# The first loads in another order, and a conv group of two blocks, in a fused convolution and gated feed-forward kernel

## The chip, the cores and the metric

One core of a Trainium2 chip runs the kernel. The metric is the device time of one execution in microseconds (us), lower is better. Times of the kernel before are the median of four runs.

## What is computed

The kernel computes a lightweight causal convolution over the sequence (seven taps, eight heads of 24 channels, softmax-normalised weights) and feeds it into a feed-forward layer whose activation is h * cos(h).

```
def _attn_ref(x, weight):                # x: 8 x 4096 x 192, weight: 8 heads x 7 taps
    w = np.exp(weight - np.max(weight, axis=-1, keepdims=True))
    w = w / (np.sum(w, axis=-1, keepdims=True) + 1e-09)
    x_pad = np.concatenate([np.zeros((B, K - 1, D)), x], axis=1)
    x_unf = x_pad[:, np.arange(S)[:, None] + np.arange(K)[None, :], :].reshape(B, S, K, H, group)
    return np.einsum('hk,bskhg->bshg', w, x_unf).reshape(B, S, D)

def _moe_ref(x, w_in, w_out):            # 32768 tokens x 192; 192 x 2048; 2048 x 192
    h = x @ w_in
    return (h * np.cos(h)) @ w_out
```

## The kernel before

**Two lanes.** The eight batch rows are split in two: lane 0 holds rows 0 to 3 in partitions 0 to 63, lane 1 rows 4 to 7 in partitions 64 to 127. A matmul of 64 rows in one lane runs beside one in the other; `lanes` (L282) interleaves two lists of such matmuls. In what follows "batch b" is the pair of rows b and b + 4.

**The convolution.** A batch has 4096 tokens, cut in 37 blocks of 112. `load_blocks` (L104 to L110) loads up to four neighbouring blocks of x, as overlapping windows of 64 tokens, into a staging tile of the pool `xw`, which has eight buffers; it issues one DMA for each lane, on the queues that it is given (SyncE's, unless said). A *conv pair* is a list of up to eight slots, each one block and one of the three chunks of 64 channels. `cast` (L157) copies the slots of a pair to bf16 (`xb`), on GpSimd unless said. `conv_first` multiplies them with the banded tap matrix (`band`), head by head: a pair whose slots are all of one chunk has 12 or 16 matmuls, one that has slots of all three chunks has 40. `evacuate` (L338, L340) copies the result to SBUF (`ct`), and `conv_out` issues a DMA transpose on SyncE (L367), which writes the conv result channel-major to `cT`. The list `pairs` gives the order of the pairs and `loads` that of the loads. Before, batch 0 is cut in groups of 5, 8, 8, 8, 8 blocks, and the others in 8, 8, 8, 8, 5. A group of eight makes three pairs, a group of five makes two; there are 56 pairs in all. Pairs 0 and 1 (the first five blocks) are transposed by TensorE (L482), not by DMA.

**The feed-forward part.** A *step* covers 512 tokens in both lanes and 128 of the 2048 hidden units. `up` (letter U) makes h from `w1` and `cT` with six matmuls in a PSUM tile `h`; `sin` (S, L387) takes the cosine on ScalarE; `mult` (M, L392) multiplies on VectorE into `g`. Sixteen steps make a tile of tokens, and steps 16 n and on read tile n. `down` (d) multiplies `g` with `w2` into the two accumulator banks `acc`, eight matmuls at a time; sixteen d make a *set* (one lane's half of a tile's output), so that there are 64 sets, with eight U in each. In a set the two lanes change banks three times. At each change a *lane mark* is needed: a memset of one element on GpSimd (L292) that waits for the d before it, and the next d waits for the mark. GpSimd works in the order in which its instructions are written, so what stands ahead of a mark on GpSimd delays it. `store` (x, y, L429) copies the accumulators out.

**The start.** The order is written out by hand. First `loads[0]` (blocks 0 to 3) and `loads[1]` (block 4), the softmax of the taps, the quarters of w_in (`load_w1`, L226 and L228, cast in L231), `loads[2]` and `loads[3]` (blocks 5 to 12), and the halves of w_out (`load_w2`, L236, cast in L241). All weights go through the same eight staging tiles. Then a string of letters is emitted by `fill`, in which each k takes the next job from the list `later()`: a cast of weights, a `cast_pair`, or a `load_ahead`. `load_ahead(n)` issues loads until the blocks of the n-th next pair are under way. With `load_ahead(4)` the loads are issued on SyncE ahead of the transposes of pairs 2, 3 and 4, which make the tokens of tile 1. Then each set is one string: `C` and `c` are the two halves of a pair's conv, `e` its copy and transposes, and `p` is `cast_pair` and `load_ahead()`. In set 1 a second pair is convolved (`CcpdMSeU`), since tile 2 needs all of pairs 5, 6 and 7.

Of the kernel before, what the change touches and what calls it, by code (L numbers as in the profile page):

```python
# [16 lines left out]
def kernel(  # L17
# [21 lines left out]
    nc = tc.nc  # L39
    B, S, D = x.shape  # L40
    H, K = weight.shape
    Dff = moe_w_in.shape[1]
# [6 lines left out]
    L = 64  # L49
    NCH = D // L  # L50
# [4 lines left out]
    NBLK = (S + W - 1) // W  # L55
# [5 lines left out]
    def dram(ap, offset, dims):  # L61
        return bass.AP(tensor=ap.tensor, offset=offset, ap=dims)
# [21 lines left out]
    def staging(dims):  # L84

        n = math.prod(dims)
        t = xw_pool.tile([128, 2 * NB * D], FP32, name="xw")[:, 0:n]
        names = "abc"[:len(dims)]
        return t.rearrange(f"p ({' '.join(names)}) -> p {' '.join(names)}", **dict(zip(names, dims)))


    lane = (slice(0, L), slice(L, 128))

    def load_blocks(b, k0, n, queues=(nc.sync, nc.sync)):

        xw = staging([2 * n, D])
        if k0 + n == NBLK:
            nc.gpsimd.memset(xw[:, 2 * n - 1, :], 0.0)
        for s, queue in enumerate(queues):
            base = ((s * HB + b) * S + k0 * W - BEFORE) * D  # L100
            w0, w1 = 0, 2 * n
            if k0 == 0:
                nc.gpsimd.memset(xw[s * L:s * L + BEFORE, 0, :], 0.0)
                queue.dma_start(out=xw[s * L + BEFORE:(s + 1) * L, 0, :], in_=dram(x, base + BEFORE * D, [[D, V], [1, D]]))  # L104
                w0 = 1
            if k0 + n == NBLK:
                w1 -= 1
                rows = TAIL - V + BEFORE
                queue.dma_start(out=xw[s * L:s * L + rows, w1, :], in_=dram(x, base + w1 * V * D, [[D, rows], [1, D]]))
            queue.dma_start(out=xw[lane[s], w0:w1, :], in_=dram(x, base + w0 * V * D, [[D, L], [V * D, w1 - w0], [1, D]]))  # L110
        for k in range(k0, k0 + n):
            xws[b, k] = xw, k - k0


    pairs = []
    loads = []
    for b in range(HB):
        five = 0 if b == 0 else NBLK - 5
        for k in range(0 if five else 5, NBLK - (5 if five else 0), 8):
            pairs += [[(b, k + j, c) for j in range(8)] for c in range(NCH)]  # L120
            loads += [(b, k, 4), (b, k + 4, 4)]
        both = [[(b, five + j, c) for c in range(2) for j in range(4)],
                [(b, five + 4, c) for c in range(NCH)] + [(b, five + j, 2) for j in range(4)]]
        if five:
            pairs += both
            loads += [(b, five, 4), (b, five + 4, 1)]
        else:
            pairs = both + pairs
            loads = [(b, five, 4), (b, five + 4, 1)] + loads
    NC = len(pairs)  # L130
    xbs = {}

# [14 lines left out]
    def cast(p, copies=(nc.gpsimd.tensor_copy,)):  # L147

        xbs[p] = xb_pool.tile([128, 8, 2, L], BF16, name="xb")
        for j, (s0, s1) in enumerate(runs(pairs[p])):  # L150
            b, k, c = pairs[p][s0]
            xw, k0 = xws[b, k]
            if s1 - s0 > 1 and pairs[p][s0 + 1][1] == k:
                src = xw[:, 2 * k0:2 * k0 + 2, :].rearrange("p w (c l) -> p c w l", l=L)
            else:
                src = xw.rearrange("p (k w) c -> p k w c", w=2)[:, k0:k0 + s1 - s0, :, c * L:(c + 1) * L]
            copies[j % len(copies)](out=xbs[p][:, s0:s1], in_=src)  # L157
# [25 lines left out]
    nc.vector.memset(band, 0.0)  # L183


    load_blocks(*loads[0])
    wmax = consts.tile([KB, H], FP32)
    nc.vector.tensor_reduce(out=wmax, in_=wq, axis=AX.X, op=ALU.max)
    nc.vector.tensor_tensor(out=wq, in0=wq, in1=wmax.unsqueeze(2).to_broadcast([KB, H, K]), op=ALU.subtract)  # L189
    wex = consts.tile([KB, H, K], FP32)  # L190
    nc.scalar.activation(out=wex, in_=wq, func=AF.Exp)  # L191
    load_blocks(*loads[1], (nc.scalar, nc.scalar))
    wsum = consts.tile([KB, H], FP32)
    nc.vector.tensor_reduce(out=wsum, in_=wex, axis=AX.X, op=ALU.add)
    nc.vector.tensor_scalar(out=wsum, in0=wsum, scalar1=1e-9, scalar2=None, op0=ALU.add)
# [23 lines left out]
    CW = Dff // NW  # L219
    staged = {}  # L220

    def load_w1(c, queue=nc.sync):

        st = staged[1, c] = staging([NCH, CW])
        cols = [1, CW]
        nc.sync.dma_start(out=st[:, 0:2], in_=dram(moe_w_in, c * CW, [[Dff, 128], [L * Dff, 2], cols]))  # L226
        for s in range(2):
            queue.dma_start(out=st[lane[s], 2], in_=dram(moe_w_in, (2 - 2 * s) * L * Dff + c * CW, [[Dff, L], cols]))  # L228

    def cast_w1(c, q, copy=nc.gpsimd.tensor_copy):  # L230
        copy(out=w1[:, q, c * CW:(c + 1) * CW], in_=staged[1, c][:, q, :])  # L231
# [6 lines left out]
    def cast_w2(c, q):  # L238
        n = NF // 2
        fs = slice(q * n // 4, (q + 1) * n // 4)  # L240
        nc.gpsimd.tensor_copy(out=w2[:, c * n:(c + 1) * n, :][:, fs, :], in_=staged[2, c][:, fs, :])  # L241

    load_w1(0, nc.scalar)
    warm = consts.tile([1, 1], FP32)
    nc.scalar.activation(out=warm, in_=wex[0:1, 0, 0:1], func=AF.Sin, bias=0.0, scale=0.0)  # L245
    load_w1(1)
# [2 lines left out]
    def load_ahead(n=2, queues=(nc.sync, nc.sync)):  # L249

        last = max(pairs[min(state["cast"] + n, NC) - 1])[:2]
        while last not in xws:
            load_blocks(*loads[state["loaded"]], queues)
            state["loaded"] += 1

    load_ahead(1)
    cast(0, (nc.vector.tensor_copy, nc.gpsimd.tensor_copy))
    cast(1, (nc.vector.tensor_copy, nc.gpsimd.tensor_copy))
    load_w1(2)
# [12 lines left out]
    def lanes(a, b, after=None):  # L272


        todo, at, ins = [list(a), list(b)], [0, 0], None
        while todo[0] or todo[1]:
            k = 0 if at[0] <= at[1] else 1
            if not todo[k]:
                k = 1 - k
            o, w, r, n, start, stop = todo[k].pop(0)  # L280
            at[k] += n
            ins = nc.tensor.matmul(out=o, lhsT=w, rhs=r, start=start, stop=stop, skip_group_check=True)  # L282
            if after is not None:
                order(ins, after)
                after = None
        return ins
# [11 lines left out]
    def cast_pair():  # L298

        if state["cast"] < NC:  # L300
            cast(state["cast"])
            state["cast"] += 1
# [18 lines left out]
    def conv_first(ps=None):  # L321

        p = state["conv"]
        state["conv"] += 1
        if ps is None:
            ps = h_pool.tile([128, 2, T], FP32, name="h")
        mms = [conv_mms(p, bank, l) for l, bank in enumerate(ps if type(ps) is list else (ps[:, 0, :], ps[:, 1, :]))]
        half = len(mms[0]) // 2
        lanes(*[m[:half] for m in mms])
        return p, ps, [m[half:] for m in mms]  # L330
# [109 lines left out]
    def emit(ops):  # L440

        for op in ops:
            if op == "C":
                if state["conv"] < NC:
                    state["open"] = conv_first(acc if count["d"] == 0 else None)
            elif op == "c":
                if "open" in state:  # L450
                    lanes(*state["open"][2])
            elif op == "p":
                cast_pair()
                load_ahead()
            elif op == "e":
                if "open" in state:
                    conv_out(*state.pop("open")[:2])
            elif op in "dt":
                down(*divmod(count[op], 16))
                count[op] += 1  # L460
            elif op in "xy":
                if count[op] < count["d"] // 16 + count["t"] // 16 - (NSETS - 1):
                    count[op] += 1
                    store("xy".index(op), count[op] - 1)
            else:
                n = count[op]
                if n < {"U": NSTEP, "S": count["U"], "M": count["S"]}[op]:
                    count[op] += 1
                    {"U": up, "S": sin, "M": mult}[op](n)
# [3 lines left out]
    for copy in (nc.scalar.copy, nc.vector.tensor_copy):  # L473
        p, ps, rest = conv_first()
# [14 lines left out]
    def later():  # L489
        yield from (lambda q=q: cast_w1(1, q) for q in range(NCH))  # L490
        yield cast_pair
        yield lambda: load_ahead(4)
        yield from (lambda q=q: cast_w1(2, q) for q in range(NCH))
        yield cast_pair
        yield cast_pair
        yield from (lambda q=q: cast_w1(3, q) for q in range(NCH))
        yield from (lambda c=c, q=q: cast_w2(c, q) for c in range(2) for q in range(4))
        yield cast_pair

    jobs = later()  # L500

    def fill(ops):

        for n, part in enumerate(ops.split("k")):
            if n:
                next(jobs)()
            emit(part)

    fill("kkkkkUSMUSMUSMkkkUSMUSMkkkUSMCceUSMkkUSMCceUSMkkkkkkkkUSMCceUSMUSMkU")
    for k in range(NSETS - 2):  # L510
        emit("dddSMdUdMSUdSdMUdSMdU" + ("CcpdMSeU" if k == 1 else "dMSU") + "dSdMCcdedMUdpSdUyxUMS")
    last = h_pool.tile([128, 2, T], FP32, name="h")
    last = [last[:, k, :] for k in range(2)]
    emit("dddMSdUdMSUdSdMUdSMdMM" + "tttt" + "dddddtttttt" + "ddxytttttt" + "xy")
# [30 lines left out]
```

## Time and profile before

| | us |
|---|---|
| median of four runs | 734.94 |
| lowest and highest run | 733.05, 735.35 |
| the profiled execution | 734.89 |
| its span, first to last instruction | 733.1 |
| TensorE matmul busy | 710.7 (97%) |
| VectorE busy | 642.0 (88%) |
| ScalarE busy | 588.9 (80%) |
| GpSimd busy | 94.8 (13%) |

In the profile PE is TensorE (PEld its weight loads), DVE is VectorE, ACT is ScalarE, POOL is GpSimd and SP is SyncE; a q after the name is the engine's sequencer, which issues DMAs. A line of a timeline gives the start from the span's beginning, the time taken, the engine, the line of the kernel, the operation with the tile written and the tiles read, the shape, the count of instructions merged in the line and, in brackets, how long the engine stood idle before it and what ended that. The granted clock of TensorE was 0.995 of full speed over the span.

### The profile page before, as it was taken

Reading aid. Unit: us, or ns where it says so; the run is one execution under the profiler, and the core shown is the slowest. Engines: PE = TensorE matmul, PEld = TensorE weight load, DVE = VectorE, ACT = ScalarE, POOL = GpSimd, SP = SyncE. Lnnn points to the kernel's source line nnn. Section 1 sums busy time; section 2 is a strip of 40 time slices with the busy share of each in tenths; the row PEclk is TensorE's granted clock in tenths of the full one; section 3 lists DMA queues with packets and bytes.
Section 4 is the critical chain, followed back from the end, with each engine's and each line's share of the span. In section 5 each row is a group of like instructions: output and inputs, shape, how many; then the busy total and the mean of one; then the engine's idle time right before and its main releaser. Section 6 shows DMA issues by size and latency. Waiting matters only on the chain.

```text
span 733.1 us, 27421 instructions
## 1 busy us (share of the span) xinstructions
PE 710.7 (97%) x12244; PEld 526.7 (72%) x12244; DVE 642.0 (88%) x594; ACT 588.9 (80%) x640; POOL 94.8 (13%) x342
## 2 busy tenths in 40 slices
PE   6669999999999999999999999999999999999997
PEld 4347777777777777777777777777777777777776
DVE  3758899899899899998998988989989999999994
ACT  3848888888888888888888888888888877787773
POOL 3511110110111111111011111011011000000000
PEclk9989999999999999999999999999999999999999
DMA  8957616455561651636543445282734211011102
GB/s 206 248 86 153 152 49 143 98 118 109 92 153 40 120 137 52 156 51 142 113 114 80 114 115 125 68 157 46 147 76 87 63 55 45 25 45 46 45 23 67
DMA packets 126210, 72.56 MB, mean 99 GB/s; under 512 B 52300, under 2 KB 124556, under 8 KB 126092
## 3 DMA queue, kind: packets, MB, share of 16 engines
q1 hardware_dynamic: 125344, 70.15, 42.8%
q8 instruction: 95, 1.56, 1.0%
q10 hardware_dynamic: 748, 0.66, 0.3%
q14 instruction: 23, 0.19, 0.1%
HBM read 33.48 MB, written 25.17 MB: 80 GB/s over the span
## 4 chain that ended last, share of the span: by engine, by line
PE 93%; DMA 4%; POOL 1%; DVE 0%; ACT 0%; issue 0%; ACTq 0%; SPq 0%; POOLq 0%
PE h L282 48%; PE acc L282 45%; DMA xw<-in_moe_w_in_dram 3%; DMA xw<-in_x_dram 1%; POOL w L231 0%; POOL xb L157 0%; DMA wq<-in_weight_dram 0%; DVE g L392 0%; ACTq L110 0%; ACT cos L387 0%; SPq L110 0%; DVE osb L429 0%; ACT osb L429 0%; ACT wex L191 0%; DVE wq L189 0%
## 5 line engine op out<-in xcount | busy, mean ns | idle before, releaser
L392 DVE TENSOR_TENSOR g<-h,cos 128x1024 bf16<-128x1024 f32 x512 | 604.3, 1220 | 38.5 <-ACT cos L387 31.6
L387 ACT ACTIVATE cos<-h 128x1024 bf16<-128x1024 f32 x512 | 511.4, 1024 | 116.3 <-PE h L282 98.5
L282 PEld LDWEIGHTS <-g 64*128 64x128 bf16 x8192 | 353.5, 94 | 109.5 <-POOL mark L292 9.3
L282 PE MATMUL acc<-w,g 64*128 64x192 bf16 x8064 | 416.1, 243 | 5.9 <-POOL mark L292 5.9
L282 PE MATMUL h<-cT,w 64*128 64x512 bf16 x3072 | 409.8, 378 | 3.1 <-DVE g L392 2.4
L282 PEld LDWEIGHTS <-w 64*128 64x128 bf16 x3072 | 147.8, 94 | 81.6 <-issue 5.8
L292 POOL MEMSET mark<- 1x1 f32 x192 | 17.1, 89 | 609.0 <-PE acc L282 600.6
L429 DVE COPY osb<-acc 128x384 f32<-128x384 f32 x63 | 35.1, 558 | 38.9 <-PE acc L282 38.9
L157 POOL CAST xb<-xw 128x512 bf16<-128x512 f32 (+1 forms) x110 | 64.6, 618 | 14.7 <-DMA xw<-in_x_dram 13.9
L340 ACT CAST ct<-h 112x1024 bf16<-112x1024 f32 (+1 forms) x52 | 52.3, 1006 | 5.5 <-PE h L282 1.8
L282 PE MATMUL h<-xb,band 64*128 64x192 bf16 (+9 forms) x872 | 34.0, 216 | 3.0 <-DVE xb L157 3.0
L282 PEld LDWEIGHTS <-band 64*128 64x128 bf16 x912 | 30.9, 95 | 7.7 <-issue 7.0
L429 ACT COPY osb<-acc 128x384 f32<-128x384 f32 x63 | 29.8, 472 | 5.7 <-PE acc L282 5.7
L231 POOL CAST w<-xw 128x512 bf16<-128x512 f32 x12 | 7.0, 616 | 6.1 <-DMA xw<-in_moe_w_in_dram 6.1
L282 PE MATMUL h<-w,g 64*128 64x192 bf16 x128 | 5.9, 243 | 0.3 <-POOL mark L292 0.3
L179 PE MATMUL acc<-unit 128*112 128x112 bf16 x46 | 4.8, 302 | 1.3 <-POOL unit L162 1.3
L179 PEld LDWEIGHTS <-unit 128*112 128x112 bf16 x46 | 4.4, 211 | 1.4 <-POOL unit L162 1.3
L282 PE MATMUL acc<-xb,band 64*128 64x192 bf16 (+2 forms) x40 | 1.9, 227 | 3.4 <-POOL xb L157 3.4
L338 ACT CAST ct<-acc 112x512 bf16<-112x512 f32 x6 | 3.2, 599 | 2.0 <-PE acc L282 2.0
L157 DVE CAST xb<-xw 128x512 bf16<-128x512 f32 (+1 forms) x2 | 1.0, 490 | 4.0 <-DMA xw<-in_x_dram 4.0
L245 ACT ACT_TABLE_LOAD x1 | 1.3, 1283 | 3.8 <-issue 3.8
L241 POOL CAST w<-xw 128x384 bf16<-128x384 f32 x8 | 3.7, 510 | 2.6 <-DMA xw<-in_moe_w_out_dram 2.6
(37 smaller groups left out, 18.9 us busy)
## 6 DMA issues: line engine op xcount, KB each, us to landing
out_dram<-osb SPq DMA_DIRECT2D x63, 384.0 KB, 2.6
xw<-in_x_dram SPq DMA_DIRECT2D x62, 384.0 KB, 6.8
xw<-in_x_dram SPq DMA_DIRECT2D x10, 336.0 KB, 4.6
xw<-in_moe_w_in_dram SPq DMA_DIRECT2D x4, 512.0 KB, 9.0
xw<-in_moe_w_out_dram SPq DMA_DIRECT2D x2, 768.0 KB
cT<-ct SPq DMA_TRANSPOSE x63, 3.2
xw<-in_moe_w_in_dram SPq DMA_DIRECT2D x6, 128.0 KB, 9.3
xw<-in_x_dram SPq DMA_DIRECT2D x8, 42.0 KB
```

Of the source, the lines that this page charges most:

```text
L157: copies[j % len(copies)](out=xbs[p][:, s0:s1], in_=src)
L179: nc.tensor.matmul(out=acc[0][0:W, 0:W], lhsT=unit, rhs=unit, start=True, stop=True)
L231: copy(out=w1[:, q, c * CW:(c + 1) * CW], in_=staged[1, c][:, q, :])
L241: nc.gpsimd.tensor_copy(out=w2[:, c * n:(c + 1) * n, :][:, fs, :], in_=staged[2, c][:, fs, :])
L245: nc.scalar.activation(out=warm, in_=wex[0:1, 0, 0:1], func=AF.Sin, bias=0.0, scale=0.0)
L282: ins = nc.tensor.matmul(out=o, lhsT=w, rhs=r, start=start, stop=stop, skip_group_check=True)
L292: ins = nc.gpsimd.memset(mark, 0.0)
L338: copy(out=ct[0:W, 0:n, s, :], in_=bank[0:W, 0:n * L].rearrange("p (j c) -> p j c", c=L))
L340: copy(out=ct[0:W, 0:n].rearrange("p j s c -> p s j c"), in_=ps[0:W, :, 0:n * L].rearrange("p s (j c) -> p s j c", c=L))
L387: nc.scalar.activation(out=cos, in_=hs[n], func=AF.Sin, bias=math.pi / 2.0, scale=1.0)
L392: nc.vector.tensor_tensor(out=g, in0=hs.pop(n), in1=cs.pop(n), op=ALU.mult)
L429: copy(out=osbs[k][:, 2 * bank:2 * bank + 2, :].rearrange("p a d -> p (a d)"), in_=src[:, 0:2 * D])
```

## The change

- `load_blocks` issues lane 1 before lane 0.
- `loads[0]` goes to SyncE (lane 0) and ScalarE (lane 1); `loads[1]`, block 4, goes to SyncE right behind it, ahead of the weights, where it was on ScalarE behind the Exp. All of the first quarter of w_in goes to SyncE, where a third of it was on ScalarE. `loads[2]` and `loads[3]` go to SyncE (lane 0) and ScalarE (lane 1), where both lanes were on SyncE.
- Batch 0 is cut in groups of 5, 8, 2, 8, 8, 6. The group of two blocks is one pair (number 5) of six slots in three chunks, the group of six makes three pairs of six slots. There are 57 pairs. With pair 5 the conv of tile 2 is complete, so the second conv of set 1 goes.
- The last `cast_pair` of `later()`, that of pair 5, goes from the end of `fill` to a `p` in set 0, behind the first lane mark and ahead of the second.
- `load_ahead(4)` in `later()` is unchanged, but the blocks that it asks for are now 13 to 22 in three loads (two, four and four blocks), where they were 13 to 20 in two.

```
-        for s, queue in enumerate(queues):
+        for s, queue in reversed(list(enumerate(queues))):
...
+    def group(b, k, n):
+        if n == 5:
+            pairs.append([(b, k + j, c) for c in range(2) for j in range(4)])
+            pairs.append([(b, k + 4, c) for c in range(NCH)] + [(b, k + j, 2) for j in range(4)])
+        elif n == 2:
+            pairs.append([(b, k + j, c) for c in range(NCH) for j in range(2)])
+        else:
+            pairs.extend([(b, k + j, c) for j in range(n)] for c in range(NCH))
+        loads.extend((b, k + j, min(4, n - j)) for j in range(0, n, 4))
+
     for b in range(HB):
...
+        for n in [8] * (NBLK // 8) + [5] if b else [5, 8, 2] + [8] * ((NBLK - 21) // 8) + [6]:
+            group(b, k, n)
+            k += n
...
-    load_blocks(*loads[0])
+    load_blocks(*loads[0], (nc.sync, nc.scalar))
+    load_blocks(*loads[1])
...
-    load_blocks(*loads[1], (nc.scalar, nc.scalar))
...
-    load_w1(0, nc.scalar)
+    load_w1(0)
...
-    load_ahead(1)
+    load_ahead(1, (nc.sync, nc.scalar))
...
-        yield cast_pair
 
     jobs = later()
...
-    fill("kkkkkUSMUSMUSMkkkUSMUSMkkkUSMCceUSMkkUSMCceUSMkkkkkkkkUSMCceUSMUSMkU")
+    fill("kkkkkUSMUSMUSMkkkUSMUSMkkkUSMCceUSMkkUSMCceUSMkkkkkkkkUSMCceUSMUSMU")
     for k in range(NSETS - 2):
-        emit("dddSMdUdMSUdSdMUdSMdU" + ("CcpdMSeU" if k == 1 else "dMSU") + "dSdMCcdedMUdpSdUyxUMS")
+        emit("dddSMdUdMSUdSdMUdSMd" + ("p" if k == 0 else "") + "UdMSUdSdMCcdedMUdpSdUyxUMS")
```

More of the change, by code (lines that the diff above doesn't have):

```diff
@@ L112, in load_blocks @@
             xws[b, k] = xw, k - k0
-    pairs = []
-    loads = []
-    for b in range(HB):
[L118 to L129, printed above, removed]
+    pairs, loads = [], []
+    def group(b, k, n):
[7 more added lines that the diff above has]
+        loads.extend((b, k + j, min(4, n - j)) for j in range(0, n, 4))
+    for b in range(HB):
+        k = 0
+        for n in [8] * (NBLK // 8) + [5] if b else [5, 8, 2] + [8] * ((NBLK - 21) // 8) + [6]:
+            group(b, k, n)
+            k += n
+        assert k == NBLK
     NC = len(pairs)
@@ L220, with load_w1 @@
     staged = {}
-    def load_w1(c, queue=nc.sync):
+    def load_w1(c):
         st = staged[1, c] = staging([NCH, CW])
@@ L227, in load_w1 @@
         for s in range(2):
-            queue.dma_start(out=st[lane[s], 2], in_=dram(moe_w_in, (2 - 2 * s) * L * Dff + c * CW, [[Dff, L], cols]))
+            nc.sync.dma_start(out=st[lane[s], 2], in_=dram(moe_w_in, (2 - 2 * s) * L * Dff + c * CW, [[Dff, L], cols]))
     def cast_w1(c, q, copy=nc.gpsimd.tensor_copy):
```

## The prediction

> **What bounds the kernel now.** I read the page first: busy time in slices, then the chain that ended last.
>
> ```profile
> PE   6669999999999999999999999999999999999997
> PEclk9989999999999999999999999999999999999999
> PE 93%; DMA 4%; POOL 1%; DVE 0%; ACT 0%; issue 0%; ACTq 0%; SPq 0%; POOLq 0%
> ```
>
> The span of 733.1 us is TensorE work; only the first three of the forty slices (18.3 us each) have holes, and the third has a lowered clock. So a change to loads and casts can win only in the first 55 us, and pays in TensorE time wherever it adds matmuls. To price that time I took GpSimd's timeline, in which the first lane mark (L292) of each set stands at a fixed place:
>
> ```profile
> 285.60 0.09 POOL L292 MEMSET mark<- 1x1 f32 x1 [2.56 <-PE acc L282]
> ...
> 296.50 0.09 POOL L292 MEMSET mark<- 1x1 f32 x1 [2.71 <-PE acc L282]
> ...
> 591.55 0.09 POOL L292 MEMSET mark<- 1x1 f32 x1 [3.83 <-PE acc L282]
> ...
> 602.01 0.09 POOL L292 MEMSET mark<- 1x1 f32 x1 [3.83 <-PE acc L282]
> ```
>
> A set without a conv pair takes 602.01 - 591.55 = 10.46 us, one with a pair of eight slots 296.50 - 285.60 = 10.90, so such a pair costs 0.44. The set from 274.50 to 285.60 holds the 40-matmul pair of a five-block group: 11.10, so 0.64. Next, the timelines of GpSimd and TensorE at the first set:
>
> ```profile
> 35.78 1.87 POOL L241 CAST w<-xw 128x384 bf16<-128x384 f32 x4 [2.58 <-DMA xw<-in_moe_w_out_dram]
> 39.01 0.62 POOL L157 CAST xb<-xw 128x512 bf16<-128x512 f32 x1 [1.35 <-DMA xw<-in_x_dram]
> 41.46 0.62 POOL L157 CAST xb<-xw 128x512 bf16<-128x512 f32 x1 [1.84 <-DMA xw<-in_x_dram]
> 42.02 0.09 POOL L292 MEMSET mark<- 1x1 f32 x1
> ```
>
> ```profile
> 35.68 0.83 PE L282 MATMUL h<-cT,w 64*128 64x512 bf16 x6
> 42.16 0.82 PE L282 MATMUL acc<-w,g 64*128 64x192 bf16 x8 [5.66 <-POOL mark L292]
> ...
> 47.63 0.81 PE L282 MATMUL h<-cT,w 64*128 64x512 bf16 x6
> ```
>
> The mark queues on GpSimd behind the two casts of conv pair 5, which wait for x blocks 13 to 20, and TensorE stands for 5.66 us. The stage table shows the consequence (columns: stage, length, busy us and count of PE, PEld, DVE, ACT, POOL, then clock, DMA share, GB/s):
>
> ```profile
> 38.00:41.00 3.00, 0.00 (x0) 0.00 (x0) 0.82 (x1) 0.00 (x0) 0.62 (x1) 0.92 1.16 125
> 41.00:44.00 3.00, 1.84 (x14) 1.02 (x16) 0.00 (x0) 0.00 (x0) 0.65 (x2) 0.50 0.84 185
> 44.00:47.00 3.00, 3.00 (x30) 1.98 (x28) 1.23 (x1) 1.16 (x2) 0.00 (x0) 0.50 0.02 5
> ```
>
> The clock is at half until 47.3. First mark to first mark of that set is 55.58 - 42.02 = 13.56 us instead of 10.90. Last, SyncE's queue:
>
> ```profile
> 25.70 7.15 SPq L110 DMA_DIRECT2D xw<-in_x_dram  x4
> 32.95 5.30 SPq L367 DMA_TRANSPOSE cT<-ct  x1
> 38.34 3.87 SPq L367 DMA_TRANSPOSE cT<-ct  x2
> ```
>
> These three transposes (conv pairs 2, 3, 4) make the tokens 512 to 1023 that up step 16 reads. A transpose usually takes SyncE 1.25 us to issue; the first two took 5.30 and 2.53 behind the four loads. Their data, copied to SBUF by 33.2, was ready; the queue ahead was not drained. DMA traffic ends between 43 and 44 (51 GB/s in that microsecond, none in the next), so the third landed at about 43.9. Step 16 is the h line at 47.63: TensorE came later than the data, so this wait is invisible today.
>
> **What the Trainium skill says.** "DMA: Bandwidth & Descriptors", section "Issuing engines are not separate DMA queues": loads issued from another engine run on the same 16 DMA engines and save only issue time. The trace agrees: the DMA share is 0.95 to 1.32 from 5 to 38 us, so moving halves of loads to ScalarE's queue creates no bandwidth. The same page, "Anatomy of one DMA": a semaphore wait happens on the issuing sequencer, so what stands behind it waits too; the 5.30 us issue agrees that SyncE is a queue in order. "TensorE: Matmul & The Clock Gate", Part 1: after an idle window of about 3.4 us, free-running, the clock halves, and a busy window restores it. The trace agrees: half clock from 40.5 to 47.3, two windows, inside a stall of 5.66.
>
> **The change, part by part.** The sum is made against the profiled execution, 734.89 us (span 733.1); the median of the four runs is 734.94, the same within 0.05.
>
> *Start.* Block 4 goes ahead of w_in. Its DVE cast waited 3.04 us and ran at 11.19, so conv pair 1 and the first up step (16.13, at once behind the w_in cast that waited 3.72) come perhaps 2 to 3 us earlier. ScalarE now issues two 42 and 336 KB loads ahead of the softmax's Exp (some 1.3 us, from SyncE's 0.59 and 0.61), and later two halves of 384 KB whose waits stand ahead of its first conv copy at 9.32; that takes perhaps 2 us of the gain back. I cost all of it at nothing: everything through the second w_out chunk is the same bytes, the DMA engines are full, and the mark cannot come before that chunk, whose casts end at 37.65. That work hides the start; were the cover gone, the bounds are 3 us of gain and 2 us of loss.
>
> *The late cast.* GpSimd no longer has pair 5's casts ahead of the first mark. The mark moves from 42.02 to about 37.7, TensorE resumes at 37.8, and the clock does not fall there, as the stall is only 1.3. Pair 5 (now blocks 13 and 14, three smaller casts) stands behind that mark and ahead of the next; its load is the first behind w_out and lands near 37.5, before the cast is reached. Its conv comes late in the set. Nothing to pay. What is late next: from the resume to step 16 TensorE has five down steps (about 0.41 each from the 0.82 of two) and two up steps (0.65 each), 3.4 us, so it asks for step 16 at 41.1.
>
> *The loads ahead of the transposes.* Before, blocks 13 to 20 (four DMAs) stood ahead of them; now blocks 13 to 22 (six DMAs, in three staging tiles). That is 2 x 192 KB = 0.39 MB more. At 290 to 235 GB/s (the rates of the stages from 25 to 35) it is 1.35 to 1.7 us, so I take the third transpose to land at 43.9 + 1.5 = 45.4, less 0.1 for x being issued from two queues at the start: 45.3. Bounds: 44.0, if the start drains 1.3 us faster; 46.8, if slower by the same. Step 16 then starts at 45.3 instead of 47.63: **2.3 us gained**; of the 6.5 that the mark offers, 4.2 go into this new wait.
>
> *The clock.* A stall of 4.2 us holds a whole window of 3.4 in (4.2 - 3.4) / 3.4, about one case in four; a nearly idle window may do as well, so I say one in three. It then costs half of some 4 to 5 us, about 2.
>
> *Conv work.* Batch 0 has groups of 5, 8, 2, 8, 8, 6 for 5 and four of 8. Before, twelve pairs at 0.44: 5.3 us. After, nine such pairs (4.0), one pair with 40 matmuls (at most the 0.64 seen; say 0.6) and three of six slots (0.33 by columns, bounds 0.3 to 0.44: 1.0): 5.6. So +0.3, on the path, as TensorE is the bound; one more ScalarE copy of about 0.8 us (1.0 for eight slots) and three more transposes (1.25 each on SyncE) lie beside it, since ScalarE is busy 85% there and SyncE mostly idle. Ends: 0 to +0.8.
>
> *The doubled conv of set 1 goes.* That set took 67.19 - 55.58 = 11.61 against 10.46 + 2 x 0.44 = 11.34: -0.3. Groups now finish one set ahead of steps 48, 96 and 144, whose transposes are issued some 8 us before use; at a usual landing of 3 to 5 us that costs nothing, and at worst about 1.
>
> Sum: -2.3 + 0.3 - 0.3 = -2.3, so 734.89 - 2.3 = 732.6; I say 732.5.
>
> **The rivals.** *(a) As reckoned*, transposes set the end and the clock holds: 731.4 to 733.5, chance 0.52. *(b) The stall simply goes*: the transposes land before 41 to 44, because the loads drain faster in the new order. In full, 47.63 - 41.1 = 6.5 gained: 728.4. For it: 1.26 us is all that the third issue needed. Against it: two transposes had to wait for fewer loads than now. 0.12. *(c) The wait takes the clock with it*: 732.5 + 2 = 734.5, no change. 0.20. *(d) Slower*: SyncE stops in front of the transposes. The third load needs a staging tile that before was not asked for so early, that of blocks 5 to 8, free when pair 4 is cast (29.7 now). If the chain of x halves from ScalarE, casts and w_in makes that cast late by over 5 us, all six loads and the transposes shift. It decides from step 16 at 49.1 at full clock (+1.5), or at about 47 with the clock lost; at 50 with the clock lost the time is 734.89 + 2.4 + 2 = 739.3. Against it: GpSimd stood idle 3.2 us for x just before, so the chain follows the DMAs, which carry the same bytes. 0.12. *(e) The change does not do what it says*: w_out's second chunk lands so late that the mark stays near 42 by itself; then only the clock is at stake, 734 to 736. 0.04.
>
> **How the numbers follow.** About 0.2% (1.5 us) is what a measurement of this kernel can tell from no change. Faster by that: nearly all of (a), (b), a little of (c): 0.63. Within it: the edge of (a), most of (c), (e): 0.22. Slower: (d) and the tail of (c): 0.15. The range leaves out the lower half of (b) and (d): 729.4 to 735.6; the likeliest case's own is 731.4 to 733.5.
>
> **What would show it.** Right: the first mark at 37 to 39; TensorE idle before step 16 for 3 to 5 us and released by a transpose; sets of 10.9 afterwards, with the last conv one set later. Wrong: no gap before step 16 (case b); a half clock behind it (c); the first mark past 41 (e); or SyncE's third load issued after 36 (d).

## The result and the profile after

| | before | after |
|---|---|---|
| median, us | 734.38 (61 runs, 730.85 to 736.85) | 731.54 (40 runs, 729.23 to 734.85) |
| profiled execution's span, us | 733.1 | 730.4 |
| first lane mark of set 0, us into the span | 42.02 | 35.26 |
| step 16 starts to finishes, us | 47.63 to 48.44 | 42.77 to 44.79 |
| first lane mark of set 1, us | 55.58 | 52.92 |

The ratio is 0.9963 with a 95% interval of 0.9956 to 0.997, 2.7 us less. The kernel before is at 734.38 over these 61 runs, 734.94 over the four of the first table. The prediction had 732.5. The sum came out, but, as the experiments show, two of its terms were wrong and cancelled.

The page of the changed kernel, busy time in slices and the chain that ended last:

```profile
PE   7779999999999999999999999999999999999997
PEclk9899999999999999999999999999999999999999
PE 94%; DMA 3%; SPq 1%; DVE 0%; POOL 0%; ACT 0%; issue 0%; POOLq 0%
```

The holes are smaller, but still all in the first three slices, and the clock still falls in them, to half from 23.4 to 30.2 and from 43.9 to 47.3. GpSimd's timeline of the changed kernel (L245 is the cast of w_out, L296 the mark, L161 the cast of x):

```profile
33.45 1.87 POOL L245 CAST w<-xw 128x384 bf16<-128x384 f32 x4 [1.97 <-DMA xw<-in_moe_w_out_dram]
35.26 0.09 POOL L296 MEMSET mark<- 1x1 f32 x1
35.30 1.09 POOL L161 CAST xb<-xw 128x256 bf16<-128x256 f32 x3
```

The casts of pair 5 now stand behind the mark and wait for nothing. Note that w_out's second chunk itself came 2.3 us sooner (33.45 instead of 35.78). TensorE's timeline at step 16, where the stall now is:

```profile
42.77 0.39 PE L286 MATMUL h<-cT,w 64*128 64x512 bf16 x2 [4.15 <-DMA cT<-ct]
43.46 0.39 PE L286 MATMUL h<-cT,w 64*128 64x512 bf16 x2 [0.30 <-DMA cT<-ct]
44.18 0.61 PE L286 MATMUL h<-cT,w 64*128 64x512 bf16 x2 [0.32 <-DMA cT<-ct]
```

Each of the three chunks of `cT` is released by its own transpose, the last at 44.18. SyncE's queue of the changed kernel shows what they stood behind, and the stage table (columns as in the prediction) what the wait did to the clock:

```profile
24.03 9.22 SPq L110 DMA_DIRECT2D xw<-in_x_dram  x6
33.34 8.79 SPq L371 DMA_TRANSPOSE cT<-ct  x3
```

```profile
38.00:42.70 4.70, 0.62 (x16) 0.39 (x10) 2.30 (x3) 1.02 (x1) 0.00 (x0) 1.00 1.30 120
...
44.00:47.30 3.30, 3.12 (x27) 2.12 (x28) 1.22 (x1) 1.58 (x2) 0.09 (x1) 0.50 0.00 0
47.30:48.00 0.70, 0.70 (x47) 0.70 (x43) 0.20 (x1) 0.47 (x1) 0.00 (x0) 1.00 0.00 0
```

TensorE stands from 38.6 to 42.77, and from 43.9 to 47.3 it works at half clock. The three transposes need 8.79 us of SyncE, where three issues of 1.25 would be under 4. The stall at the mark is gone, and a stall at step 16 has taken its place.

### The profile page after: what moved, and what is told of

The parts are those of the page before. It is cut to its first block, busy times and chain, and to the rows that moved or that the text cites. A ratio compares the mean times of both kernels' runs of the same rounds, so it can differ in the third digit from the quotient of the medians.

```text
span 730.4 us, 27515 instructions
## 1 busy us (share of the span) xinstructions
PE 711.8 (97%) x12284; PEld 526.6 (72%) x12284; DVE 641.6 (88%) x594; ACT 589.4 (81%) x641; POOL 95.4 (13%) x345
## 4 chain that ended last, share of the span: by engine, by line
PE 94%; DMA 3%; SPq 1%; DVE 0%; POOL 0%; ACT 0%; issue 0%; POOLq 0%
PE h L286 49%; PE acc L286 46%; DMA xw<-in_moe_w_in_dram 3%; DMA cT<-ct 1%; SPq L110 1%; DVE g L396 0%; ACT cos L391 0%; POOL w L235 0%; POOL xb L161 0%; SPq L371 0%; DVE osb L433 0%; ACT osb L433 0%; SPq L104 0%; POOLq L543 0%; POOL mark L296 0%
## 5 line engine op out<-in xcount | busy, mean ns | idle before, releaser
L296 POOL MEMSET mark<- 1x1 f32 x192 | 17.1, 89 | 610.6 <-PE acc L286 602.0
L161 POOL CAST xb<-xw 128x512 bf16<-128x512 f32 (+1 forms) x113 | 64.9, 606 | 10.3 <-DMA xw<-in_x_dram 9.2
L344 ACT CAST ct<-h 112x1024 bf16<-112x1024 f32 (+2 forms) x53 | 52.5, 990 | 9.1 <-PE h L286 5.5
L286 PE MATMUL h<-xb,band 64*128 64x192 bf16 (+10 forms) x912 | 34.1, 214 | 0.0
L245 POOL CAST w<-xw 128x384 bf16<-128x384 f32 x8 | 3.7, 510 | 2.0 <-DMA xw<-in_moe_w_out_dram 2.0
```

Source lines behind the costliest of these rows:

```text
L296: ins = nc.gpsimd.memset(mark, 0.0)
L344: copy(out=ct[0:W, 0:n].rearrange("p j s c -> p s j c"), in_=ps[0:W, :, 0:n * L].rearrange("p s (j c) -> p s j c", c=L))
```

## The experiments

My theory after seeing this: the end of the start-up is set by the three transposes, which wait in SyncE's queue behind the loads of blocks 13 to 22; the new order of the first loads makes all of this come a little sooner. Rivals: the new start is the whole gain; it is hidden; or the order on SyncE doesn't matter and DMA bytes decide. Ratios are to the kernel before on the same chip. The new start, the groups and the late cast are named as in the section on the change.

| run | what it has | median, us | ratio (95%) |
|---|---|---|---|
| e1_start_only | new start | 730.58 | 0.9947 (0.9928 to 0.9967) |
| e2_old_start | new groups, late cast | 734.89 | 0.9999 (0.9989 to 1.0008) |
| e3_late_cast_only | late cast | 733.58 | 0.998 (0.9971 to 0.9989) |
| e4_transposes_first | all, transposes ahead of the loads | 724.99 | 0.9868 (0.9852 to 0.9883) |
| e5_x_halves_only | halves of blocks 5 to 12 on ScalarE's queue | 735.59 | 1.0014 (1.0002 to 1.0027) |
| e6_head_only | the rest of the new start | 729.88 | 0.9939 (0.9919 to 0.9959) |
| e7_kept_warm | all, TensorE kept busy in the stall | 730.38 | 0.9945 (0.9927 to 0.9963) |
| e8_old_groups_transposes_first | new start, old groups, late cast, transposes first | 730.52 | 0.9938 (0.9915 to 0.9961) |
| e9_w_in_on_sync | w_in's first quarter on SyncE | 733.10 | 0.9973 (0.9962 to 0.9985) |
| e10_block4_ahead | block 4 ahead on SyncE | 731.33 | 0.9953 (0.9936 to 0.997) |
| e11_blocks_0_3_split | blocks 0 to 3 split, lane 1 first | 733.07 | 0.998 (0.997 to 0.999) |
| e12_old_start_transposes_first | new groups, late cast, transposes first | 728.14 | 0.9905 (0.9888 to 0.9921) |

### Which part carries the gain: e1, e2, e3

e1 is the kernel before with the edits of the new start (all the lines shown below for e5, e9, e10 and e11); e2 is the changed kernel with these undone; e3 is the kernel before with the last job of `later()` moved:

```
-        yield cast_pair
...
-    fill("...USMCceUSMUSMkU")
+    fill("...USMCceUSMUSMU")
...
-        emit("dddSMdUdMSUdSdMUdSMdU" + ...
+        emit("dddSMdUdMSUdSdMUdSMd" + ("p" if k == 0 else "") + "U" + ...
```

> The kernel before with only the new start: queues, lane order, block 4 ahead of the weights; groups and the late cast as before. Theory (step 16 is served when the third transpose lands, and the new start makes all loads land about 1 us sooner): the mark still stands behind pair 5's casts, but these come 1 to 2 us sooner, so 1 to 2 us less than before, 732.5 to 733.5. Rival 'the start is the whole gain': 731.5, as the changed kernel. Rival 'the start is hidden': 734.4, no change.

> The changed kernel with the old start: groups 5, 8, 2, 8, 8, 6 and the late cast alone. Theory: ten blocks of loads stand ahead of the transposes, and without the new start the third lands about 45.4 us into the span; about 1.1 us slower than the changed kernel, 732.6. Rival 'the start is hidden': the same as the changed kernel, 731.5. Rival 'the start is the whole gain': 734.4.

> The kernel before with the cast of pair 5 moved behind the first mark, and nothing else: eight blocks of loads stay ahead of the transposes. Theory: the mark comes at about 37.7, the transposes land at 43.9 as before, step 16 starts at about 44 instead of 47.6, and some 1.5 us of half clock are paid behind it: 732 to 732.5. Rival 'the two-block group is what removes the stall': the cast now waits for blocks 13 to 20 ahead of the second mark, TensorE stands there until 42 and little is gained, 734.

The start alone gives 0.53%, some 3.9 us, as much as the whole change within the intervals. Groups and late cast without it give nothing, to 0.1%; beside it they add no gain that these intervals show (0.9947 without them, 0.9963 with them). In e1's profile the first mark still stands behind pair 5's casts, but at 38.27 instead of 42.02, and TensorE waits 4.89 us for it instead of 5.66:

```profile
38.42 0.58 PE L282 MATMUL acc<-w,g 64*128 64x192 bf16 x8 [4.89 <-POOL mark L292]
```

So the rival "the start is the whole gain" won on the times, and my theory, which gave the start 1 to 2 us and the rest 1.8, missed on both. e2's trace shows where the removed stall went. GpSimd's mark, TensorE's step 16, SyncE's queue and a stage of e2:

```profile
37.85 0.09 POOL L296 MEMSET mark<- 1x1 f32 x1
```

```profile
45.44 0.61 PE L286 MATMUL h<-cT,w 64*128 64x512 bf16 x2 [4.33 <-DMA cT<-ct]
```

```profile
25.75 10.55 SPq L110 DMA_DIRECT2D xw<-in_x_dram  x6
36.39 8.42 SPq L371 DMA_TRANSPOSE cT<-ct  x3
```

```profile
45.40:47.30 1.90, 1.69 (x8) 0.45 (x10) 0.00 (x0) 0.00 (x0) 0.00 (x0) 0.50 0.59 129
47.30:51.70 4.40, 4.40 (x80) 3.63 (x78) 2.45 (x2) 2.38 (x3) 0.09 (x1) 0.50 0.00 0
```

The mark came at 37.85, but the first transpose released step 16 only at 45.44 and the third at 46.83, with half clock from 44.9 to 51.8. Before, step 16 began at 47.63 with the clock just restored at 47.3. What the mark gave, the wait and the clock took.

e3, with the old groups and so two DMAs fewer ahead of the transposes, keeps 1.5 us by its ratio; I had expected about 2. Its second mark did not wait for blocks 13 to 20, as the rival had it: the casts were done at 44.1 and the mark came at 48.37. But its profiled execution took 735.26 us, well above its median, and its third transpose came as late as e2's (step 16's last matmuls started at 46.99), so where the 1.5 us come from is not shown.

### Is it the order on SyncE: e4 and e12

```
-        yield lambda: load_ahead(4)
+        yield lambda: load_ahead(3)
```

That is all of e4 against the changed kernel, and of e12 against e2. Every engine's order stays, except that SyncE issues the three transposes ahead of the loads of blocks 15 to 22.

> The changed kernel with load_ahead(3) in place of load_ahead(4) in the list of jobs, so that SyncE issues the loads of blocks 15 to 22 behind the three transposes instead of ahead of them. Theory (the transposes wait for the queue ahead of them): they land by about 38, step 16 starts without a stall at 38.6 instead of 42.8 to 44.2, the clock does not halve behind it; 5 to 6 us faster than the changed kernel, 725.5 to 726.5. Rival 'DMA bytes decide, not the order' or 'transposes are slow beside loads': they land at 42 or later, at most 1 us gained, 730.5. Rival 'pair 6 is late': its cast waits at the end of set 0 and holds the marks of set 1, so half of the gain is lost, 728.5.

> The changed kernel with the old start and with the transposes ahead of the loads of blocks 15 to 22 (load_ahead(3)). With the transposes out of the way only the chunk of w_out holds the first mark. Theory (the start is then worth what it moves that chunk, 32.1 against 35.8, and no more): the mark at 37.7 instead of 34.5, 3 to 3.7 us slower than with the new start, 728 to 728.7. Rival (the start gains only through the transposes): 725 to 726. Rival (the old start costs more, as a longer wait at the mark lets the clock fall): 730 or more.

e4 takes 724.99 us, 6.5 less than the changed kernel (7.0 by the ratios), and is the fastest version here: "DMA bytes decide" has fallen. SyncE, TensorE and GpSimd in e4:

```profile
23.84 4.17 SPq L110 DMA_DIRECT2D xw<-in_x_dram  x2
28.10 5.79 SPq L371 DMA_TRANSPOSE cT<-ct  x3
33.98 2.66 SPq L110 DMA_DIRECT2D xw<-in_x_dram  x4
```

```profile
37.23 0.84 PE L286 MATMUL acc<-w,g 64*128 64x192 bf16 x16
37.89 0.83 PE L286 MATMUL h<-cT,w 64*128 64x512 bf16 x6
```

```profile
34.54 0.09 POOL L296 MEMSET mark<- 1x1 f32 x1 [0.52 <-PE acc L286]
...
44.66 0.62 POOL L161 CAST xb<-xw 128x512 bf16<-128x512 f32 x1 [2.28 <-DMA xw<-in_x_dram]
45.56 0.09 POOL L296 MEMSET mark<- 1x1 f32 x1 [0.28 <-PE acc L286]
```

The transposes are all issued by 33.9, step 16 (37.89) follows the down steps without a gap, and the set takes 45.56 - 34.54 = 11.02 us. The loads that were moved back still serve: the cast of pair 6 waited 2.28 us for them, 0.3 ahead of the next mark.

e12 came out as the theory had it, at 728.1 (five runs, 727.53 to 728.59). With the transposes out of the way the new start is worth some 3 us (3.1 by these medians, 2.7 by the ratios), about as much as it moves w_out's second chunk: 32.15 in e4, and in e12

```profile
34.97 1.86 POOL L245 CAST w<-xw 128x384 bf16<-128x384 f32 x4 [0.81 <-DMA xw<-in_moe_w_out_dram]
```

### Is the two-block group needed: e8

e8 is e1 with the late cast, behind the second mark of set 0, and with blocks 13 to 20 loaded behind the transposes.

```
-        yield lambda: load_ahead(4)
+        yield lambda: None
...
-        yield cast_pair
...
-    fill("...USMCceUSMUSMkU")
+    fill("...USMCceUSMUSMU")
+    load_ahead(1)
...
-        ... ("CcpdMSeU" if k == 1 else "dMSU") ...
+        ... ("CcpdMSeU" if k == 1 else "dpMSU" if k == 0 else "dMSU") ...
```

> The new start with the old groups (5, 8, 8, 8, 8), the loads of blocks 13 to 20 issued behind the three transposes, and pair 5 cast behind the second mark of set 0. It asks whether the two-block group is needed once the transposes go first. Theory: blocks 17 to 20 land at about 40, their cast ends at 41, the conv of pair 5 is due at 40.2: a stall of about 1 us, 0.3 us less conv, 0.3 more in set 1; 725.5 to 726.5 against 725.0 with the group. Rival 'the group carries the gain': 728 or more. Rival 'the group only costs': 724.7.

It took 730.5, 5 us more than e4. GpSimd and TensorE in e8:

```profile
42.85 0.61 POOL L157 CAST xb<-xw 128x512 bf16<-128x512 f32 x1 [2.64 <-DMA xw<-in_x_dram]
```

```profile
43.52 0.72 PE L282 MATMUL h<-xb,band 64*128 64x192 bf16 x12 [3.12 <-POOL xb L157]
43.99 1.52 PE L282 MATMUL acc<-w,g 64*128 64x192 bf16 x16
```

Blocks 17 to 20 landed at 42.8, not 40, and TensorE stood 3.12 us, with half clock behind it (16 down matmuls in 1.52 us instead of 0.84). So, in this order of loads, the group is what lets the transposes go first: its pair needs only two blocks, which can stay ahead of them. In the changed kernel this was not used. Old groups with some of blocks 13 to 20 ahead of the transposes, or with pair 5 convolved later, were not tried.

### What in the start does it: e5, e6, e9, e10, e11

Each is the kernel before with one of these pieces; e6 is e1 without the piece of e5.

```
e5
-    load_ahead(1)
+    load_ahead(1, (nc.sync, nc.scalar))
e9
-    load_w1(0, nc.scalar)
+    load_w1(0)
e10
     load_blocks(*loads[0])
+    load_blocks(*loads[1])
...
-    load_blocks(*loads[1], (nc.scalar, nc.scalar))
e11
-        for s, queue in enumerate(queues):
+        for s, queue in reversed(list(enumerate(queues))):
...
-    load_blocks(*loads[0])
+    load_blocks(*loads[0], (nc.sync, nc.scalar))
```

> The kernel before with one line of the new start: the loads of blocks 5 to 12 put lane 1 on ScalarE's queue; all else as before. Theory Q (the loads land sooner because bytes stand in a second queue beside SyncE's, so more are outstanding in the first 20 us): most of the gain of the whole start, 731 to 732, and w_out's second chunk cast at 32 to 33.5 instead of 35.8. Rival O (the order of the first loads does it): 734.5 to 735, chunk at 35.8.

> The rest of the new start: blocks 0 to 3 from two queues, block 4 ahead of the weights, the first quarter of w_in wholly on SyncE, lane 1 first; the loads of blocks 5 to 12 stay on SyncE. Theory Q: little, 734 to 735, chunk at 35 to 35.8. Rival O: most of the gain of the whole start, 731 to 732, chunk at 32 to 33.5.

> The kernel before with one word of the new start: the third part of the first quarter of w_in goes to SyncE instead of ScalarE. Theory W (ScalarE's two w_in pieces land only at 14.3 and 15.3, and SyncE, whose DMAs reuse their semaphores, stands behind them from 11.9 to 14.3): SyncE issues its loads up to 2 us sooner, w_out's second chunk is cast at 32 to 33.5 instead of 35.8, 730 to 731.5. Rivals B (block 4's place) and H (the split of blocks 0 to 3): 734 to 735, chunk at 35 to 36.

> The kernel before with only block 4 moved: from ScalarE's queue behind the Exp to SyncE's, ahead of the weights. Theory W: w_in's pieces stay on ScalarE and may even go out sooner there; 733.5 to 735, chunk at 34.5 to 36. Rival B: 730 to 731.5, chunk at 32 to 33.5.

> The kernel before with only blocks 0 to 3 split over both queues and lane 1 issued first. Theory W: 734 to 735, chunk at 35 to 36. Rival H (the first bytes start sooner, and everything behind them): 731 to 732.5, chunk at 33 to 34.

A second queue for the large loads gives nothing, or a little less than nothing, in agreement with the Trainium skill, "DMA: Bandwidth & Descriptors", section "Issuing engines are not separate DMA queues". The head of the start gives all of it (0.61%). Of its three moves each gives a part: 0.27, 0.47 and 0.20%, by the medians together more than the whole, so they probably overlap. w_in on SyncE and the split of blocks 0 to 3 are each less than the whole; for block 4 that is not shown, as e10's interval overlaps that of e6.

The traces show what the head changes. DMA share and GB/s (the last two columns) by stage, kernel before and then e1:

```profile
2.00:8.00 6.00, 4.58 (x49) 4.33 (x48) 3.28 (x10) 1.92 (x3) 0.98 (x4) 1.00 0.79 205
8.00:14.00 6.00, 3.04 (x76) 2.50 (x75) 1.77 (x4) 1.76 (x4) 2.35 (x4) 1.00 1.00 246
14.00:20.00 6.00, 5.29 (x27) 1.91 (x29) 2.44 (x5) 2.81 (x4) 2.29 (x4) 1.00 1.11 228
20.00:28.00 8.00, 4.36 (x43) 2.02 (x42) 6.42 (x6) 6.61 (x8) 3.54 (x7) 1.00 1.07 245
```

```profile
2.00:8.00 6.00, 3.76 (x52) 3.59 (x52) 3.54 (x11) 3.02 (x4) 1.75 (x5) 1.00 0.92 227
8.00:14.00 6.00, 5.59 (x93) 3.92 (x94) 2.60 (x4) 2.42 (x4) 3.28 (x6) 0.50 1.08 285
14.00:20.00 6.00, 4.00 (x28) 1.50 (x25) 5.33 (x5) 5.38 (x6) 1.23 (x2) 0.93 1.11 219
20.00:28.00 8.00, 5.93 (x66) 3.49 (x67) 4.09 (x4) 5.01 (x8) 5.86 (x11) 0.79 1.07 316
```

From 20 to 28 us the share is 1.07 in both, and the rate 245 in one and 316 in the other. That is not a rate that only e1 reaches: the kernel before moves 367 GB/s from 29.0 to 31.3, at a share of 1.09, and e1 moves 358 from 25 to 28. SyncE's w_out loads are issued at 19.2 and 21.0 in e1 instead of 22.3 and 24.1, and the fast stretch comes with them. The lead is older than that. By the rates of these tables e1 has moved 0.13 MB more at 8 us, 0.37 at 14, 0.31 at 20 and 0.88 at 28, and in the first stage the share was still under 1 (0.79, in e1 0.92).

One thing that holds SyncE back at the start is on record in the kernel before: the fourth load of blocks 5 to 12 is issued only at 14.29, after a wait of 2.4 us for a piece of w_in that ScalarE had issued. The line is of SyncE's waits up to 75 us (total, count, longest):

```profile
SPq L110 <- DMA xw<-in_moe_w_in_dram: 4.9, 3, 2.4
```

In e9 the same four loads go out without such a gap, from 7.68 to 11.85, as its theory said, but it gained 0.27% instead of the 0.4 to 0.6% expected. In e10, which left those pieces on ScalarE, they go out from 9.00 to 11.95 as well, in an execution of 734.93 us. So this wait alone does not make the gain, and how the three moves share it stays open. e10's profiled execution is far from its median of 731.33 (its w_out chunk was cast at 35.94), so I draw nothing else from it.

### The price of the clock: e7

```
+        if n == NF:
+            idle = h_pool.tile([128, 2, T], FP32, name="h")
+            for _ in range(82):
+                nc.tensor.matmul(out=idle[0:W, 0, 0:W], lhsT=unit, rhs=unit, start=True, stop=True)
         h = h_pool.tile([128, 2, T], FP32, name="h")
```

> The changed kernel with 82 extra matmuls ahead of up step 16, into an h tile that nothing reads (some 4 us of TensorE, in the stall before that step); the outputs stay those of the kernel. Theory (part of the stall's price is the half clock behind it): the clock stays at full, the set after is 1.4 to 2 us shorter, 729.5 to 730.5 against 731.5 of the changed kernel. Rival (the clock costs nothing that the stall doesn't): 731.5, or up to 0.5 more if the extra matmuls outlast the stall.

e7's stages, with the extra matmuls from 42.12 to 46.56 in this execution:

```profile
42.00:47.00 5.00, 5.00 (x94) 4.58 (x90) 1.23 (x1) 0.60 (x1) 0.00 (x0) 1.00 0.69 84
47.00:51.00 4.00, 4.00 (x106) 3.17 (x104) 2.36 (x2) 2.99 (x4) 0.80 (x4) 1.00 0.02 4
```

The clock stays at full through the wait. The ratio is 1.3 us better than that of the changed kernel, close to what was expected, but the intervals (0.9927 to 0.9963 and 0.9956 to 0.997) overlap, so the price is likely and not settled. The profiled execution is the slowest of e7's eight (733.48), and in it the extra matmuls outlast the loads and transposes, whose traffic ends at 45, so that step 16 starts only at 46.50. The half clock itself, one window of 3.4 us in the changed kernel (43.9 to 47.3) and two in e2 (44.9 to 51.8), agrees with "TensorE: Matmul & The Clock Gate", Part 1, of the skill.

## Why the prediction came out

- **The bound and the stall at the mark: right.** From the first mark of set 1 to the end, the kernel before takes 677.5 us and the changed one 677.5; what was gained, was gained ahead of it (the two conv terms below cancel).
- **The start, costed at nothing: wrong.** By the ratios it is worth 2.7 us between e2 and the changed kernel, 2.7 between e12 and e4, and 3.9 alone (e1). The step that failed is "the DMA engines are full, and the mark cannot come before that chunk". The chunk was the right limit for the mark, but it moved by 2.3 us in the profile, and the third transpose behind it by 2.65 (46.83 in e2, 44.18 in the changed kernel). I read a DMA share near 1 as a ceiling on bytes; it is not, as 245 and 316 GB/s at the same 1.07 show. Even the 3 us of gain that I named as a bound was meant for TensorE's first steps, not for the loads.
- **The late cast, 2.3 us gained: wrong.** With the old start the mark came at 37.85 as forecast, and the last down steps before step 16 ended at 41.1 as forecast, but e2 gained nothing. The next two terms say why.
- **The transposes next: right in mechanism, too small in size.** Forecast 45.4 with the old start, measured 46.83 (e2); 44.18 in the changed kernel, with the new. I priced 0.39 MB of loads at their own rate and left the issue of the third transpose at the 1.26 us of before; with more ahead, it took 2.1 us as well (44.81 - 42.70 in e2). The section "Anatomy of one DMA" of the Trainium skill, "DMA: Bandwidth & Descriptors", which I named, speaks of semaphore waits; the 5.30 us were issue time with the data ready, and what holds the issue no run here shows. A wait of that kind is the one of 2.4 us above, at 14.29.
- **The clock, one chance in three: probably too low.** In the profiles of e2, of e3 and of the changed kernel, one execution each, it fell during the wait. By estimate it took about 1.4 us in the changed kernel (half of 44.56 to 47.3), against the 2 that I had given to case (c).
- **Conv work, +0.3: right.** Set 0 of e4 takes 11.02, so the 40-matmul pair costs 0.56 (forecast 0.6). The three sets with six-slot pairs take 10.73, 10.88 and 10.79 in the changed kernel, 1.02 in all over three bare sets (forecast 1.0).
- **The doubled conv of set 1, -0.3: right.** Set 1 takes 10.90 instead of 11.61, of which 0.44 is the pair that moved. No later step waited for a transpose.

By parts, I had -2.3 for groups and cast and 0 for the start. The runs gave 0 (within 0.8) and -2.7. That the two sums agree is luck. The signs that I had named say so too: the first mark came at 35.26, ahead of the 37 to 39 of the likeliest case, and the half clock of case (c) was there, while the time fell just inside the range of case (a).

## What to carry to other kernels

When a stall is removed, look up on which queue the next operand stands, and count what is ahead of it there: here six loads stood ahead of three transposes, and moving four of those loads behind them gave 6.5 us, more than twice what the change gave. A busy share of the DMA engines near 1 is no proof that the order of the loads doesn't matter; compare bytes moved by a given time. And test each part of a change alone, even when the total agrees with the forecast.

## What I had not expected of the hardware

The same DMA share (1.07) went with 245 and with 316 GB/s. A DMA transpose that takes SyncE 1.25 us to issue took 4.28, 2.17 and 2.16 us behind queued loads. With two of the six loads ahead instead (e4) the three took 2.41, 1.93 and 1.25.
